# Attention and two feed-forward layers on one core: other PSUM banks, sums spread by TensorE, low halves on VectorE, weights from 16-bit halves

## The chip, the cores and the metric

The kernel runs on 1 core of one Trainium2 chip. The metric is the device time of one execution in microseconds (us); a run gives the median of several executions.

## The reference

```python
scores = scale * np.matmul(q, k.transpose(0, 1, 3, 2))        # 2 x 8 x 768 x 768, D = 64
keep = is_global | is_local                                   # 8 global keys, 96 local ones
scores = np.where(keep, scores - slopes * dist, -1000000000.0)
a = np.exp(scores - np.max(scores, axis=-1, keepdims=True))
a = a / (np.sum(a, axis=-1, keepdims=True) + 1e-09)
x = (a @ v)                                                   # as 1536 tokens x 512
h = x @ w_in                                                  # 512 x 2048
x = (np.maximum(h, 0) + np.log1p(np.exp(-np.abs(h)))) @ w_out # layer 0, 2048 x 512
h = x @ w_in2
out = (h / (1 + np.exp(-1.702 * h))) @ w_out2                 # layer 1
```

The weights of the two layers come as 64-bit doubles. Products are made of fp32 values split in a high and a low part: high by high, high by low and low by high.

## The kernel before

**Attention** goes over 12 blocks of 128 queries (n), each in two halves of 4 heads (g = 0, 1), so 24 halves s. `split_attention` is a loop of ns + 3 = 27 iterations whose order is written out by hand: each engine runs its instructions in the order in which the code issues them. Iteration s works on four halves at once:

- TensorE (PE): the scores of s + 1; in odd iterations `turn_r`, the turned 1/sum of a block; `turn`, the transposes of the weights of s - 1; the turned k or q of block n + 2; `values`, the product with v of s - 2. So an iteration runs from one start of scores to the next.
- VectorE (DVE): `reduce(s + 1)`, which adds the bias to the scores and takes their minimum; the low parts kl (even) and ql (odd); in even iterations `weigh` (1/sum, L503 and L504) of block n - 1 and `normalise` (output by 1/sum, L519) of block n - 2 with the high part of x (L526); steps of the converter.
- ScalarE (ACT): the high parts kh and qh, the exponentials of s (`weights_of`), and the copies out of PSUM: turned weights (`copy_p`, L587) and 1/sum (`copy_r`, L514).
- GpSimd (POOL): 1/sum spread over 64 columns (L506), the low part of x (L527), and moves within kh and kl.

Even iterations are those with g = 0. In this text block n of attention is "a block of queries" and a slice of the weights "a weight block".

**The eight PSUM banks** during attention before: four that rotate (`h_pool`, scores take two at a time and the feed-forward layer one), two for the turned weights, one for the outputs (`ps_o`), one for turned q, k and 1/sum (`ps_q`).

**The converter** puts together the fp32 high and low parts of the weights from the doubles, 32 weight blocks of 128 x 1024, by the steps of `split`: t (L142), its scaling on ScalarE (L144), the remaining bits `rest` (L146, L148), the sign (L152), the high part w (L156 on VectorE for the first six weight blocks, L159 on ScalarE for the others), a mask (L160), and the low part (L162). `pump` issues steps while a budget lasts; during attention, with `later` set, ScalarE's part waits in `hold` until the end of an iteration or the next step that empties it. Weight blocks 0 to 5 of layer 0 are put together during attention, the others in layer 0 and 1.

**The feed-forward layers** are 96 units of 12 matmuls into h (`first`) and 12 into four accumulators (`second`), `bend` between them. The first unit's matmuls stand inside attention's last iterations, in four pieces (chunks).

## Time and profile before

| | |
|---|---|
| median of 3 runs | 653.48 us (653.38 to 653.83) |
| profiled execution | 654.91 us, its span 653.3 us |
| PE busy | 623.5 us of the span |
| DVE busy | 411.0 us |
| ACT busy | 362.4 us |
| POOL busy | 50.7 us |

Busy time is an average over stages with different limits, so the rows below cut the span where the work changes: the attention loop, its end, and the layers. A row of the timeline has the start, the length, the operation with what it writes and reads, and in brackets how long the engine was idle before it and what released it. An operation's length holds some overlap with the next one on its engine, so what one costs in a busy engine is the distance from its start to the next one's start.

### The profile page before, as it was taken

Reading aid. Unit: us, or ns where it says so; the run is one execution under the profiler, and the core shown is the slowest. Engines: PE = TensorE matmul, PEld = TensorE weight load, DVE = VectorE, ACT = ScalarE, POOL = GpSimd, SP = SyncE. Lnnn points to the kernel's source line nnn. Section 1 sums busy time; section 2 is a strip of 40 time slices with the busy share of each in tenths; the row PEclk is TensorE's granted clock in tenths of the full one; section 3 lists DMA queues with packets and bytes.
Section 4 is the critical chain, followed back from the end, with each engine's and each line's share of the span. In section 5 each row is a group of like instructions: output and inputs, shape, how many; then the busy total and the mean of one; then the engine's idle time right before and its main releaser. Section 6 shows DMA issues by size and latency. Waiting matters only on the chain.

```text
span 653.3 us, 8758 instructions
## 1 busy us (share of the span) xinstructions
PE 623.5 (95%) x3290; PEld 508.1 (78%) x3290; DVE 411.0 (63%) x752; ACT 362.4 (55%) x676; POOL 50.7 (8%) x70
## 2 busy tenths in 40 slices
PE   7889788899999999999999999999999999999995
PEld 4677676688788778888888888888888888888884
DVE  5988978989999976899867997674121111211111
ACT  4988997576887666777666763443222222222221
POOL 3224442100000000000000003000000000000000
PEclk9899999999999999999999999999999999999998
DMA  9877657950100001530005671000010000100002
GB/s 227 160 187 172 127 142 230 330 205 0 65 1 2 0 1 64 194 130 0 1 0 194 207 245 65 0 1 0 1 65 0 1 1 1 64 2 0 1 1 70
DMA packets 65715, 51.51 MB, mean 79 GB/s; under 512 B 41920, under 2 KB 58304, under 8 KB 65664
## 3 DMA queue, kind: packets, MB, share of 16 engines
q1 hardware_dynamic: 65376, 50.86, 26.5%
q8 instruction: 28, 0.46, 0.3%
q14 instruction: 23, 0.19, 0.1%
q10 hardware_dynamic: 288, 0.00, 0.0%
HBM read 44.70 MB, written 4.19 MB: 75 GB/s over the span
## 4 chain that ended last, share of the span: by engine, by line
PE 74%; DVE 18%; ACT 4%; issue 3%; DMA 1%; ACTq 0%; DVEq 0%
PE h L238 33%; PE acc L292 20%; PE acc L290 13%; DVE t L152 2%; PE t L580 2%; DVE w L162 2%; PE s L543 2%; PE o L602 2%; PE qps L461 2%; DVE g L252 2%; DVE gl L259 1%; DVE pr L556 1%; DVE rest L146 1%; DVE rest L148 1%; DVE g L246 1%
## 5 line engine op out<-in xcount | busy, mean ns | idle before, releaser
L259 DVE TENSOR_TENSOR gl<-g,gh 128x512 fp32r<-128x512 f32 x96 | 67.1, 699 | 165.7 <-ACT gh L257 165.6
L290 PE MATMUL acc<-gh,w 128*128 128x512 f32 x384 | 126.6, 390 | 0.0
L292 PE MATMUL acc<-w,gh 128*128 128x512 f32 x384 | 125.5, 389 | 0.0
L257 ACT ACTIVATE gh<-g 128x512 fp32r<-128x512 f32 x96 | 60.4, 629 | 93.9 <-PE acc L292 80.0
L290 PEld LDWEIGHTS acc<-gh,w 128*128 128x128 f32 x384 | 72.1, 188 | 15.5 <-ACT e L269 0.3
L292 PEld LDWEIGHTS acc<-w,gh 128*128 128x128 f32 x384 | 72.1, 188 | 14.9
L265 ACT ACTIVATE g<-h 128x512 f32<-128x512 f32 x48 | 28.7, 598 | 93.8 <-PE h L238 76.2
L290 PE MATMUL acc<-gl,w 128*128 128x512 f32 x192 | 74.9, 390 | 0.6 <-DVE gl L259 0.6
L292 PE MATMUL acc<-w,gl 128*128 128x512 f32 x192 | 74.8, 390 | 0.0
L268 ACT ACTIVATE e<-h 128x512 f32<-128x512 f32 x48 | 28.4, 592 | 33.8 <-PE h L238 30.8
L238 PE MATMUL h<-x0h,w 128*128 128x512 f32 x128 | 44.8, 406 | 2.4 <-DVE g L254 2.4
L568 ACT ACTIVATE pr<-pr,mins 128x256 f32<-128x256 f32 (+1 forms) x96 | 45.7, 484 | 1.2 <-DVE mins L556 1.2
L238 PE MATMUL h<-x1h,w 128*128 128x512 f32 x128 | 42.7, 393 | 0.6 <-DVE g L254 0.6
L144 ACT ACTIVATE t<-t,ebias 128x1024 int32<-128x1024 int32 x32 | 36.7, 1146 | 10.9 <-DVE t L142 10.8
L290 PEld LDWEIGHTS acc<-gl,w 128*128 128x128 f32 x192 | 36.0, 188 | 8.6 <-DVE gl L259 1.2
L292 PEld LDWEIGHTS acc<-w,gl 128*128 128x128 f32 x192 | 36.0, 188 | 8.0 <-DVE gl L259 0.5
L238 PE MATMUL h<-x2h,w 128*128 128x512 f32 x128 | 42.0, 389 | 0.0
L238 PE MATMUL h<-y1h,w 128*128 128x512 f32 x128 | 42.0, 389 | 0.0
L238 PE MATMUL h<-y2h,w 128*128 128x512 f32 x128 | 42.0, 389 | 0.0
L238 PE MATMUL h<-y0h,w 128*128 128x512 f32 x128 | 42.0, 389 | 0.0
L148 DVE SCALAR_TENSOR_TENSOR rest<-raw,rest 128x1024 int32<-128x1024 int32 x32 | 39.8, 1245 | 0.2
L246 DVE SCALAR_TENSOR_TENSOR g<-c,g 128x512 f32<-128x512 f32 x48 | 32.8, 684 | 10.7 <-ACT g L272 10.7
(125 smaller groups left out, 1150.6 us busy)
## 6 DMA issues: line engine op xcount, KB each, us to landing
raw<-in_moe_w_in SPq DMA_DIRECT2D x32, 512.0 KB, 4.8
raw<-in_moe_w_out SPq DMA_DIRECT2D x32, 512.0 KB, 5.6
kn<-in_k SPq DMA_DIRECT2D x12, 256.0 KB, 4.3
qn<-in_q SPq DMA_DIRECT2D x12, 256.0 KB, 4.7
vn<-in_v SPq DMA_DIRECT2D x12, 256.0 KB, 3.4
out<-o SPq DMA_DIRECT2D x12, 256.0 KB, 2.1
vp<-vn SPq DMA_DIRECT2D x10, 192.0 KB, 3.8
part<-o SPq DMA_DIRECT2D x2, 512.0 KB, 2.8
```

What stands on the lines that cost most here:

```text
L144: s["hold"].append(lambda: nc.scalar.activation(t, t, AF.Relu, bias=ebias, scale=float(2 ** 12)))
L148: nc.vector.scalar_tensor_tensor(rest, low, 17, rest, op0=ALU.logical_shift_right, op1=ALU.bitwise_or)
L152: nc.vector.scalar_tensor_tensor(t, top, -2 ** 31, t, op0=ALU.bitwise_and, op1=ALU.bitwise_or)
L238: nc.tensor.matmul(h, lhsT=w[:, a, c * P:(c + 1) * P], rhs=b[:, c, :], start=c == 0 and n == 0, stop=c == KD - 1 and n == 2)
L246: nc.vector.scalar_tensor_tensor(st[u - 1]["g"], st[u - 1]["c"], -1.0, st[u - 1]["g"], op0=ALU.add, op1=ALU.subtract)
L257: nc.scalar.activation(gh, g, AF.Copy)
L259: nc.vector.tensor_tensor(gl, g, gh.bitcast(F32), op=ALU.subtract)
L265: nc.scalar.activation(g, s["h"], AF.Gelu_apprx_sigmoid)
L268: nc.scalar.activation(e, s["h"], AF.Abs)
L290: nc.tensor.matmul(o, lhsT=wo[:, a, ms], rhs=g, **kw)
L292: nc.tensor.matmul(o, lhsT=g[:, ms], rhs=wo[:, a, :], **kw)
L568: nc.scalar.activation(pr[:, j, e, :w], pr[:, j, e, :w], AF.Exp, bias=mins[:, H * n + h:H * n + h + 1], scale=-1.0, accum_out=sums[n][:, h ...
```

## The change

- **PSUM.** The four rotating banks become four named ones, h0 to h3, one buffer each. Scores use h0 and h1 every time, before one pair of four in turn. Turned q, k and 1/sum use h2 and h3 in turn. The bank set free goes to `ps_o`, which has two. The layers' h goes through the four in the order of `BANKS`.
- **Sums.** 1/sum is no longer spread by GpSimd and then turned with 4 transposes; 8 matmuls of TensorE do both, with 1/sum broadcast over 64 columns against the identity.
- **Low half of x** on VectorE. `normalise` with both halves of x stands ahead of `weigh`, kl and `reduce`, and behind the converter's first steps.
- **Weights.** `rest` is put together by two operations, each writing one 16-bit half of a word. The high part w is copied by ScalarE for all weight blocks. In attention a step that needs ScalarE's result is issued only after the `flush` at the end of an iteration. The declared costs are 640 for 680.
- `reduce(0)` stands ahead of the loop; the first unit's chunks are issued in three iterations, not four; the last iterations' budget is half.

```diff
+BANKS = (2, 0, 1, 3)
...
     def split(s):
         raw = s.pop("raw")
-        top, low = raw[:, :, 1], raw[:, :, 0]
+        top, half = raw[:, :, 1], raw.bitcast(U16).rearrange("p m (two h) -> p m two h", two=2)
         t = conv.tile([P, NW2], I32, tag="t", name="t")
         nc.vector.tensor_scalar(t, top, 0x7FFFFFFF, 9, op0=ALU.bitwise_and, op1=ALU.logical_shift_right)
-        yield 680
+        yield 640
         s["hold"].append(lambda: nc.scalar.activation(t, t, AF.Relu, bias=ebias, scale=float(2 ** 12)))
         rest = conv.tile([P, NW2], I32, tag="t", name="rest")
-        nc.vector.tensor_scalar(rest, top, 0x1FF, 15, op0=ALU.bitwise_and, op1=ALU.logical_shift_left)
-        yield 680
-        nc.vector.scalar_tensor_tensor(rest, low, 17, rest, op0=ALU.logical_shift_right, op1=ALU.bitwise_or)
-        yield 1210
-        while s["hold"]:
-            s["hold"].pop()()
+        part = rest.bitcast(U16).rearrange("p (m h) -> p m h", h=2)
+        nc.vector.tensor_scalar(part[:, :, 0], half[:, :, 0, 1], 0xFFFF, None, op0=ALU.bitwise_and)
+        yield 640
+        nc.vector.tensor_scalar(part[:, :, 1], half[:, :, 1, 0], 0x1FF, None, op0=ALU.bitwise_and)
+        yield 640
+        yield None
         nc.vector.scalar_tensor_tensor(t, top, -2 ** 31, t, op0=ALU.bitwise_and, op1=ALU.bitwise_or)
         w = s["pool"].tile([P, 2, NW2], F32R, tag=s["tag"], name=s["name"])
+        s["hold"].append(lambda: nc.scalar.activation(w[:, 0, :], t.bitcast(F32), AF.Copy))
         yield 1210
-        if s["early"]:
-            nc.vector.tensor_copy(w[:, 0, :], t.bitcast(F32))
-            yield 640
-        else:
-            nc.scalar.activation(w[:, 0, :], t.bitcast(F32), AF.Copy)
+        yield None
         nc.vector.tensor_scalar(t, t, -2 ** 23, None, op0=ALU.bitwise_and)
-        yield 680
-        nc.vector.scalar_tensor_tensor(w[:, 1, :], rest, 2.0 ** -35, t.bitcast(F32), op0=ALU.mult, op1=ALU.mult)
+        yield 640
+        nc.vector.scalar_tensor_tensor(w[:, 1, :], rest, 2.0 ** -36, t.bitcast(F32), op0=ALU.mult, op1=ALU.mult)
         s["w"] = w
         yield 1210
...
         def run(self):
             while self.queue:
                 yield from split(self.queue.pop(0))
+            yield 0
         def step(self):
-            cost = next(self.ops, None)
+
+            if self.stuck and self.hold:
+                return None
+            self.stuck = False
+            cost = next(self.ops, 0)
+            if cost == 0:
+                self.ops = self.run()
+                cost = next(self.ops)
             if cost is None:
-                self.ops = self.run()
-                cost = next(self.ops, None)
+                self.stuck = True
+                return self.step()
             if not self.later:
                 self.flush()
             return cost
...
             self.credit += budget
             while self.credit > 0:
                 cost = self.step()
+                if cost is None:
+                    break
                 self.credit = self.credit - cost if cost else 0
         def flush(self):
             while self.hold:
-                self.hold.pop()()
+                self.hold.pop(0)()
         def finish(self, s):
             while "w" not in s:
-                self.step()
+                if self.step() is None:
+                    self.flush()
     def ffn_phase(x1, slots, work, h_pool, weights, converter):
...
                 if u not in st:
-                st[u] = {"h": h_pool.tile([P, TB], F32, tag="h", name="h")}
+                st[u] = {"h": h_pool.tile([P, TB], F32, tag=f"h{BANKS[u % 4]}", name="h")}
             h = st[u]["h"]
             for c in chunks:
                 for n, (a, b) in enumerate(((0, xh), (0, xl), (1, xh))):
...
         ps_t = pool("ps_t", 1, space=PSUM)
-        ps_o = pool("ps_o", 1, space=PSUM)
-        ps_q = pool("ps_q", 1, space=PSUM)
+        ps_o = pool("ps_o", 2, space=PSUM)
+        turns = []
...
                 nc.sync.dma_start(t[WIN:P], v[b, :, 0:GLB, :].rearrange("h p d -> p h d"))
                 vs[n].insert(0, t)
-        def turned(src, early=False):
-            t = (ps_o if early else ps_q).tile([P, NP, P], F32, tag="o" if early else "q", name="qps")
+        def bank(last=False):
+
+            turns.append(h_pool.tile([P, TB], F32, tag=f"h{3 if last else 2 + len(turns) % 2}", name="qps"))
+            return turns[-1].rearrange("p (c k) -> p c k", c=NP)
+
+        def turned(src):
+            t = bank()
             src = src.rearrange("p h d -> p (h d)")
             for p in range(NP):
                 nc.tensor.transpose(t[:, p, :], src[:, p * P:(p + 1) * P], ident)
...
             nc.vector.tensor_scalar(sums[n], sums[n], 1e-9, None, op0=ALU.add)
             nc.vector.reciprocal(sums[n], sums[n])
-            r = s_pool.tile([P, H, D], F32, tag="r", name="r", bufs=1)
-            nc.gpsimd.tensor_scalar(r, sums.pop(n).to_broadcast([P, H, D]), 1.0, 1.0, op0=ALU.mult, op1=ALU.mult)
-            rts[n] = r
         def turn_r(n):
-            rts[n] = turned(rts[n])
+
+            r = sums.pop(n)
+            t = rts[n] = bank(n >= nb - 3)
+            for p in range(NP):
+                for e in range(2):
+                    nc.tensor.matmul(t[e * D:(e + 1) * D, p, :], lhsT=r[:, 2 * p + e, :].to_broadcast([P, D]),
+                                     rhs=ident, start=True, stop=True)
         def copy_r(n):
-            rt = s_pool.tile([P, NP, P], F32, tag="rt", name="rt", bufs=1)
-            nc.scalar.activation(rt, rts[n], AF.Copy)
-            rts[n] = rt
+            y = s_pool.tile([P, NP, P], F32, tag="y", name="y")
+            nc.scalar.activation(y, rts[n], AF.Copy)
+            rts[n] = y
         def normalise(n):
-            y = ys[n] = rts.pop(n)
-            nc.vector.tensor_tensor(y, outs.pop(n), y, op=ALU.mult)
-
-        def split_x(n):
             b, i = blocks[n]
             t0 = b * S + i * P
             hi, lo = (x[:, :, t0 % TB:t0 % TB + P] for x in x1[t0 // TB])
-            y = ys.pop(n)
+            y = rts.pop(n)
+            nc.vector.tensor_tensor(y, outs.pop(n), y, op=ALU.mult)
             nc.vector.tensor_copy(hi, y)
-            nc.gpsimd.tensor_tensor(lo, y, hi.bitcast(F32), op=ALU.subtract)
+            nc.vector.tensor_tensor(lo, y, hi.bitcast(F32), op=ALU.subtract)
...
             i = blocks[n][1]
             w, at = (NW, own(i) - WIN - GLB) if i else (P, own(0))
             qh, ql = qts[n]
-            banks = [h_pool.tile([P, TB], F32, tag="h", name=f"s{e}") for e in range(2)]
+            banks = [h_pool.tile([P, TB], F32, tag=f"h{e}", name=f"s{e}") for e in range(2)]
             ps[s] = ([x.rearrange("p (j k) -> p j k", j=2) for x in banks], w)
             for j in range(2):
                 for m, (a, c) in enumerate(((qh, kh), (qh, kl), (ql, kh))):
...
         yield
         scores(0)
         spin(2)
+        reduce(0)
         for s in range(ns + 3):
             n, g = divmod(s, 2)
             live = n < nb
...
                 turn(s - 1)
             if s == 0:
-                reduce(0)
                 bias(bias_0, d0, 4)
                 weights_of(0)
                 run(split_k(1), split_q(1))
...
                     weights_of(s)
                 if s == 1:
                     bias(bias_w, dw, 4)
+                if s > 1:
+                    converter.pump(budget // 2)
+                if g == 0 and 0 <= n - 2 < nb:
+                    normalise(n - 2)
                 if g == 0 and 0 <= n - 1 < nb:
                     weigh(n - 1)
-                if s > 1:
-                    converter.pump(budget // 2)
                 run(kept)
                 if s + 1 < ns:
                     reduce(s + 1)
                 if s == 4:
                     check_counts()
-                if g == 0 and 0 <= n - 2 < nb:
-                    normalise(n - 2)
-                    split_x(n - 2)
+                converter.pump(budget // 2 * g if s + 1 < ns else budget)
                 if g == 1 and 0 <= n - 1 < nb:
                     copy_r(n - 1)
-                converter.pump(budget // 2 * g if s + 1 < ns else 2 * budget)
                 if s >= 1 and s - 1 < ns:
                     copy_p(s - 1)
             converter.flush()
...
             if s >= 2 and s - 2 < ns:
                 values(s - 2)
-            if ns - 5 <= s < ns - 1:
-                first(0, [s - ns + 5])
+            if ns - 4 <= s < ns - 1:
+                first(0, ((0,), (1,), (2, 3))[s - ns + 4])
             if ns - 1 <= s < ns + 2:
                 bend(s - ns + 1)
                 if s < ns + 1:
```

**Place 1: VectorE in the even iteration s = 8.** The rows start at the first step of it that is not a reduction; of the eight rows of `reduce` (L556 before, L570 after) one stands. Before (s_747 are scores, o the output in PSUM, rest, t and raw_1 the converter's tiles, x0h and x0l the halves of x):

```order
L148 SCALAR_TENSOR_TENSOR rest<-raw_1_291,rest 128x1024 [waits DVE_49]
L503 TENSOR_SCALAR sum<-sum 128x8 [waits Activation_49]
L504 RECIPROCAL sum<-sum 128x8 [waits DVE_49]
L490 TENSOR_TENSOR kl<-qps,kh 128x4x128 [waits Activation_49]
L556 ISA pr,mins<-s_747,bias_w 128x256 [waits PE_49]
...
L519 TENSOR_TENSOR rt<-o,rt 128x512 [waits Pool_49]
L526 CAST x0h<-rt 128x4x128 [waits DVE_49]
L152 SCALAR_TENSOR_TENSOR t<-raw_1_291,t 128x1024
```

After:

```order
L158 TENSOR_SCALAR t<-t 128x1024 [waits Activation_49]
L160 SCALAR_TENSOR_TENSOR w_1_723<-rest,t 128x1024 [waits DVE_49]
L539 TENSOR_TENSOR y<-o,y 128x512 [waits PE_49]
L540 CAST x0h<-y 128x4x128 [waits DVE_49]
L541 TENSOR_TENSOR x0l<-y,x0h 128x4x128 [waits DVE_49]
L517 TENSOR_SCALAR sum<-sum 128x8
L518 RECIPROCAL sum<-sum 128x8 [waits DVE_49]
L504 TENSOR_TENSOR kl<-qps,kh 128x4x128 [waits Activation_49]
L570 ISA pr,mins<-s_753,bias_w 128x256 [waits PE_49]
```

`normalise` (L519, now L539) went from behind the reduction to ahead of it, with the low half (L541) behind it, and the converter's mask (L158) and low part (L160) of weight block 1, which the order before reaches later, stand ahead of all; the mask waits for ScalarE.

**Place 2: ScalarE at the end of s = 6 and in s = 7.** Before:

```order
L476 ACTIVATE qh<-qps 128x512 [waits PE_49]
L568 ACTIVATE pr,sum<-pr,mins 128x256 [waits DVE_49] x4
L514 ACTIVATE rt<-qps 128x512 [waits PE_49,Pool_49]
L587 ACTIVATE pt<-t 128x1024 [waits PE_49,Activation_49]
L144 ACTIVATE t<-t,ebias 128x1024
L488 ACTIVATE kh<-qps 128x4x128 [waits PE_49]
L568 ACTIVATE pr,sum<-pr,mins 128x256 [waits DVE_49] x4
```

After (y is 1/sum in SBUF, w_1_723 the high part of weight block 1):

```order
L490 ACTIVATE qh<-qps 128x512 [waits PE_49]
L582 ACTIVATE pr,sum<-pr,mins 128x256 [waits DVE_49] x4
L531 ACTIVATE y<-qps 128x512 [waits PE_49]
L601 ACTIVATE pt<-t 128x1024 [waits PE_49,Activation_49]
L155 ACTIVATE w_1_723<-t 128x1024 [waits DMAHW4_49,DMAHW3_49,DVE_49]
L502 ACTIVATE kh<-qps 128x4x128 [waits PE_49]
L582 ACTIVATE pr,sum<-pr,mins 128x256 [waits DVE_49] x4
```

In s = 7 the scaling of t stood between the copy of the turned weights (pt) and kh; now the copy of w (L155) stands there, and the scaling is earlier.

**Place 3: VectorE at the end of attention**, ahead of the first units' bends (g and e). Before:

```order
L142 TENSOR_SCALAR t<-raw_5_1631 128x1024 [waits DMAHW2_49,DMAHW1_49]
L146 TENSOR_SCALAR rest<-raw_5_1631 128x1024
L148 SCALAR_TENSOR_TENSOR rest<-raw_5_1631,rest 128x1024 [waits DVE_49]
L246 SCALAR_TENSOR_TENSOR g<-c,g 128x512 [waits Activation_49]
L152 SCALAR_TENSOR_TENSOR t<-raw_5_1631,t 128x1024 [waits Activation_49]
L156 CAST w_5_1814<-t 128x1024 [waits DVE_49]
L160 TENSOR_SCALAR t<-t 128x1024 [waits DVE_49]
L162 SCALAR_TENSOR_TENSOR w_5_1814<-rest,t 128x1024 [waits DVE_49]
L246 SCALAR_TENSOR_TENSOR g<-c,g 128x512 [waits Activation_49]
L252 SCALAR_TENSOR_TENSOR g<-g,e 128x512
L252 SCALAR_TENSOR_TENSOR g<-g,e 128x512 [waits DVE_49]
L254 SCALAR_TENSOR_TENSOR g<-h,g 128x512 [waits DVE_49] x2
```

After:

```order
L153 SCALAR_TENSOR_TENSOR t<-raw_5_1406,t 128x1024 [waits Activation_49]
L158 TENSOR_SCALAR t<-t 128x1024 [waits Activation_49]
L160 SCALAR_TENSOR_TENSOR w_5_1748<-rest,t 128x1024 [waits DVE_49]
L539 TENSOR_TENSOR y<-o,y 128x512 [waits PE_49,Activation_49]
L540 CAST x2h<-y 128x4x128 [waits DVE_49]
L541 TENSOR_TENSOR x2l<-y,x2h 128x4x128 [waits DVE_49]
L517 TENSOR_SCALAR sum<-sum 128x8
L518 RECIPROCAL sum<-sum 128x8 [waits DVE_49]
L255 SCALAR_TENSOR_TENSOR g<-c,g 128x512 [waits Activation_49] x2
L261 SCALAR_TENSOR_TENSOR g<-g,e 128x512 [waits DVE_49] x2
L263 SCALAR_TENSOR_TENSOR g<-h,g 128x512 [waits DVE_49] x2
```

Before, the whole of weight block 5 (raw_5) stands here; after, its last three steps, and three operations on x.

## Rows read from the trace of the kernel before

**Rows 1.** Stages: from:to, length, busy us (instructions) per engine, granted PE clock, DMA.

```profile
27.85:106.24 78.39, 66.90 (x735) 55.26 (x733) 67.61 (x227) 68.81 (x194) 30.17 (x35) 1.00 0.66 159
106.24:128.98 22.74, 18.62 (x148) 14.88 (x147) 21.60 (x40) 14.09 (x30) 4.88 (x4) 1.00 0.92 310
128.98:133.09 4.11, 4.11 (x12) 3.02 (x12) 2.81 (x6) 4.11 (x8) 1.16 (x1) 0.58 0.55 208
133.09:235.00 101.91, 100.69 (x439) 81.52 (x438) 99.63 (x139) 74.04 (x111) 0.12 (x1) 1.00 0.12 42
235.00:645.50 410.50, 410.45 (x1810) 339.23 (x1808) 199.72 (x271) 183.79 (x283) 5.94 (x4) 1.00 0.15 50
```

**Rows 2.** TensorE in time, one odd and one even half: start, us, operation, idle before.

```profile
32.75 0.39 PE L543 MATMUL s<-kh,qh 64*128 64x256 f32 x2
...
33.67 0.66 PE L461 MATMUL qps<-ident,r 128*128 128x128 f32 x4
34.16 1.04 PE L580 MATMUL t<-ident,pr 128*128 128x128 f32 x8
...
36.68 0.39 PE L543 MATMUL s<-kh,qh 64*128 64x256 f32 x2
...
37.59 1.09 PE L580 MATMUL t<-ident,pr 128*128 128x128 f32 x8
...
39.94 0.44 PE L602 MATMUL o<-pt,vp 128*64 128x128 f32 x4 [0.81 <-PE qps L461]
...
40.96 0.39 PE L543 MATMUL s<-kh,qh 64*128 64x256 f32 x2
```

**Rows 3.** VectorE in time, in the even half.

```profile
36.29 0.16 DVE L503 TENSOR_SCALAR sum<-sum 128x8 f32<-128x8 f32 x1
...
36.61 0.65 DVE L142 TENSOR_SCALAR t<-raw 128x1024 int32<-128x1024 int32 x1
37.18 0.68 DVE L490 TENSOR_TENSOR kl<-qps,kh 128x512 fp32r<-128x512 f32 x1
37.78 0.41 DVE L556 CUSTOM_DVE_ANT_0 pr<-s,bias_w 128x256 f32<-128x256 f32 x1
...
39.15 0.68 DVE L519 TENSOR_TENSOR rt<-o,rt 128x512 f32<-128x512 f32 x1
39.87 0.43 DVE L526 CAST x0h<-rt 128x512 fp32r<-128x512 f32 x1
40.21 0.68 DVE L146 TENSOR_SCALAR rest<-raw 128x1024 int32<-128x1024 int32 x1
```

**Rows 4.** GpSimd in time, in the same even half.

```profile
40.38 1.66 POOL L527 TENSOR_TENSOR x0l<-rt,x0h 128x512 fp32r<-128x512 f32 x1 [2.12 <-DVE x0h L526]
```

**Rows 5.** VectorE by line while layer 0 runs: count, busy, mean ns, idle.

```profile
L148 DVE SCALAR_TENSOR_TENSOR rest<-raw,rest 128x1024 int32<-128x1024 int32 x10 | 12.2, 1217 | 0.0
...
L142 DVE TENSOR_SCALAR t<-raw 128x1024 int32<-128x1024 int32 x10 | 6.8, 682 | 0.0
```

**Rows 6.** ScalarE by line: the later weight blocks' copy.

```profile
L159 ACT ACTIVATE w<-t 128x1024 fp32r<-128x1024 f32 x10 | 10.6, 1056 | 2.2 <-DVE t L152 1.8 <-DVE rest L148 0.4
```

**Rows 7.** ScalarE in time, in the odd half.

```profile
34.42 0.60 ACT L514 ACTIVATE rt<-qps 128x512 f32<-128x512 f32 x1 [0.96 <-PE qps L461]
35.30 1.03 ACT L587 ACTIVATE pt<-t 128x1024 f32<-128x1024 f32 x1 [0.28 <-PE t L580]
36.22 0.59 ACT L488 ACTIVATE kh<-qps 128x512 fp32r<-128x512 f32 x1
```

**Rows 8.** TensorE in time, in the first halves.

```profile
15.12 0.63 PE L461 MATMUL qps<-ident,qn 128*128 128x128 f32 x4 [1.70 <-DVE mins L556]
```

**Rows 9.** TensorE in time: the first product after attention.

```profile
128.98 0.50 PE L238 MATMUL h<-x0h,w 128*128 128x512 f32 x1 [2.42 <-DVE g L254]
```

**Rows 10.** TensorE in time: a wait in layer 0.

```profile
229.37 0.50 PE L290 MATMUL acc<-gl,w 128*128 128x512 f32 x1 [0.58 <-DVE gl L259]
```

**Rows 11.** Granted clock in short stretches, columns as in the first group.

```profile
16.00:18.00 2.00, 1.94 (x16) 0.75 (x12) 1.52 (x6) 1.98 (x9) 0.00 (x0) 0.69 1.15 333
18.00:20.00 2.00, 2.00 (x10) 1.67 (x10) 1.97 (x9) 0.87 (x2) 0.00 (x0) 0.50 1.40 226
```

**Rows 12.** TensorE in time: one wait in the loop.

```profile
31.73 0.44 PE L602 MATMUL o<-pt,vp 128*64 128x128 f32 x4 [1.45 <-issue]
```

More of the change, by code (lines that the diff above doesn't have):

```diff
@@ L12 @@
 I32 = mybir.dt.int32
-U32 = mybir.dt.uint32
+U16 = mybir.dt.uint16
 AF = mybir.ActivationFunctionType
@@ L128, in load_words, with load_weights @@
                           sources[l][1].bitcast(I32)[f * P:(f + 1) * P, :])
-    def load_weights(pool, l, f, early=False):
+    def load_weights(pool, l, f):
         raw = pool.tile([P, NW2, 2], I32, tag=f"w{f}", name=f"raw{l}_{f}")
         load_words(raw, l, f)
-        return {"raw": raw, "pool": pool, "tag": f"w{f}", "name": f"w{l}_{f}", "early": early}
+        return {"raw": raw, "pool": pool, "tag": f"w{f}", "name": f"w{l}_{f}"}
     def split(s):
         raw = s.pop("raw")
-        top, low = raw[:, :, 1], raw[:, :, 0]
+        top, half = raw[:, :, 1], raw.bitcast(U16).rearrange("p m (two h) -> p m two h", two=2)
@@ L171, in __init__ @@
             self.queue, self.ops, self.credit, self.blocks, self.hold = [], iter(()), 0, [], []
-            self.later = later
+            self.later, self.stuck = later, False
         def add(self, s):
@@ L436, in split_attention @@
         raw, qts, vs = {}, {}, {}
-        ps, prs, pts, outs, sums, rts, ys = {}, {}, {}, {}, {}, {}, {}
+        ps, prs, pts, outs, sums, rts = {}, {}, {}, {}, {}, {}
         def load(n):
@@ L469, in turn_q @@
         def turn_q(n):
-            qts[n] = turned(raw[n]["qn"], n < 2)
+            qts[n] = turned(raw[n]["qn"])
         def split_q(n):
@@ L485, in split_k @@
             i = blocks[n][1]
-            t = raw[n]["kn"]
+            t = raw.pop(n)["kn"]
             at = slice(own(i), own(i) + P)
@@ L814, in hidden_pool @@
     def hidden_pool(hctx):
-        return hctx.enter_context(tc.tile_pool(name="h", bufs=4, space=PSUM, reuse_waits="tile"))
+        return hctx.enter_context(tc.tile_pool(name="h", bufs=1, space=PSUM, reuse_waits="tile"))
     with ExitStack() as wctx:
@@ L831, in attention_two_ffns @@
                     f = len(weights)
-                    weights[0, f] = load_weights(wa_pool, 0, f, early=True)
+                    weights[0, f] = load_weights(wa_pool, 0, f)
                     converter.add(weights[0, f])
```

## Prediction

> **What bounds the kernel now.** I read the stages first [rows 1], cut at starts of scores. From 235 to 645.5 TensorE is busy 410.45 of 410.50 us: nothing here shortens its matmuls, so that stage stays. From 133.09 to 235 VectorE is busy 99.63 of 101.91 us beside TensorE's 100.69: nearly a tie, in which VectorE makes TensorE wait now and then. From 106.24 to 128.98 TensorE is busy 18.62 of 22.74 and VectorE 21.60: VectorE bounds, with weight blocks left over. The short stage behind it runs at a granted clock of 0.58 of full speed. The loop, 78.39 us, has no full engine (PE 66.90, DVE 67.61, ACT 68.81), so there the chain of waits counts. It holds iterations 4 to 21, nine even and nine odd: 4.36 us each on average.
>
> Then the timeline of TensorE [rows 2]. The odd iteration from 32.75 has no wait and takes 3.93 us. The even one from 36.68 takes 4.28, of which 0.81 is a wait ahead of `values`. The row names the turned q as releaser, but `normalise` on VectorE (L519) runs from 39.15 to 39.83 [rows 3], 0.11 before `values` start: the single output bank is the cause. TensorE's own even work is 4.28 - 0.81 = 3.47.
>
> **The change part by part.** *Two output banks* take away the 0.81, if nothing else ends last. *One pair of banks for scores* puts another wait there: scores of s + 2 need `reduce(s + 1)` finished, where before VectorE could be an iteration late. In even iterations `reduce` now has `normalise`, both halves of x, `weigh` and kl ahead of it, and `normalise` can't start before the last `values`, which end as the iteration starts. By distances of starts [rows 3]: `normalise` 0.72, high half 0.34, `weigh` 0.32, kl 0.60, reduction 1.37. The low half leaves GpSimd, where it takes 1.66 [rows 4]; on VectorE I take kl's 0.60, the same kind of subtraction (bounds 0.60 and the 0.72 of `normalise`). The sum is 3.95, and with two hand-overs between engines of 0.11 to 0.2 some 4.3: as long as now. TensorE's 3.47 lies beside it, so the gain of the second bank is used up. Nine pairs of 3.93 + 4.3 are 74.1 us; what 78.39 holds above that is converter work.
>
> *The sums* take 8 matmuls of 64 columns for 4 transposes (33.67 to 34.16, 0.49) [rows 2]. Sixteen of the same width in `values` take 40.96 - 39.94 = 1.02, so 8 take 0.51: nothing (bounds 0 and 0.5 in each odd iteration, 4.5 in all, if each costs as much as a transpose). The spread on GpSimd that is removed lay beside other work. Turned q, k and sums in two banks, and the layers' order of four banks: nothing, since each bank is read by ScalarE and VectorE within an iteration and comes back two turns later; without that cover a turn would wait, at most by the 0.6 of a copy.
>
> *The weights.* `rest` was L146, of L142's form, and L148: 0.68 + 1.22 [rows 5]. Now it is two operations of one source on 16-bit halves with a step. No row shows such a one: between 0.68 (like L142, one source from SBUF) and 1.22 (like L148, one element per cycle), a little of either end thinkable. I take 0.68, as they are L142's kind with the same count of elements: 0.54 saved per weight block. The copy of w leaves VectorE in attention (about L142's 0.65) for ScalarE, 1.06 [rows 6]. A page on this: the Trainium skill, VectorE: DVE Perf Modes, "What auto-detection actually checks", has values packed only at a step of one, but two ports for a single source in SBUF; by that the operation costs what L142 costs, and the sum would be the same.
>
> *The new wait in the loop.* ScalarE's copy of w comes behind the copy of the turned weights at an odd iteration's end, ahead of kh (place 2 of the change), and the mask (L158) heads VectorE's next even iteration (place 1). In the odd iteration of [rows 7] the turned weights wait for TensorE (0.28) and kh starts at 36.22: the copy would end at 36.22 + 1.06 = 37.28, 0.60 after the even iteration starts at 36.68; where ScalarE is later, up to 0.9. I take 0.75 (bounds 0 and 0.9). Behind the mask stand `normalise`, `weigh`, kl and `reduce`, and TensorE's scores wait for all of these. With the mask's 0.57 (as L142, 36.61 to 37.18) `normalise` starts at 1.32 in place of some 0.15: 1.2 late, in iterations 12, 16 and 20. In 4 and 8 the low part of w (1.22) stands ahead too: 2.4 late. Together 3 x 1.2 + 2 x 2.4 = 8.4 (bounds 0 and 10). One of two chunks of the first unit in the loop stands in an odd iteration, against which nothing waits: three matmuls, 0.7. The loop is then 74.1 + 8.4 + 0.7 = 83.2, **+4.8**.
>
> *Ahead of the loop* TensorE waits 1.70 for the first reductions [rows 8]; `reduce(0)` now stands earlier: **-1.0** (0 to -1.7).
>
> *The end of attention.* Since the loop has taken in more weight steps, place 3 shows 3 steps of weight block 5 (1.22 + 0.68 + 1.22 = 3.1) where 7 stood (6.4 by these durations, the copy at 0.65); weight block 4 is wholly ahead. Low halves add 0.6 each. So VectorE no longer bounds, and the 22.74 - 18.62 = 4.1 of TensorE's idle time goes, of which 2.42 stands ahead of the second unit [rows 9]: **-4.1** (bounds -2 and -4.1). The 4.11 us at 0.58 follow that wait: 4.11 x 0.42 = 1.7 of full clock are lost, **-1.7** (0 to -1.7).
>
> *Layer 0.* TensorE's idle time is 101.91 - 100.69 = 1.22, or, at the next stage's 410.5 / 1810 us per record, 101.91 - 439 x 0.2268 = 2.35; one wait on VectorE is 0.58 [rows 10]. Ten weight blocks at 0.54 free 5.4 us of VectorE: **-1.5** (0 to -2.4). Layer 1: nothing, VectorE is half idle.
>
> *The clock.* The five lengthened even iterations leave TensorE idle for 4.3 + 1.2 - 3.47 = 2.0, or 3.2. After 1.70 at the start it ran at 0.69 and 0.50 [rows 11], after 2.42 at 0.58, after 1.45 in the loop [rows 12] at 1.00 [rows 1]. I take it that the two of 3.2 lower the clock and the three of 2.0 don't, for the work around them is dense. One costs 1.7 at most; the next even iteration has 0.8 of slack, which covers half a microsecond of it: 1.25 each, **+2.5** (bounds 0 and 5 x 1.7 = 8.5). The Trainium skill, TensorE: Matmul & The Clock Gate, "HAM oscillation — how this bites in real kernels", says that a wait which comes back in every round puts the array to half clock each time, and so speaks against this change; the row of 1.45 at 1.00 shows that a shorter one in this loop does not, and no row here has one of 2.0 in it.
>
> **Sum.** 4.8 - 1.0 - 4.1 - 1.7 - 1.5 + 2.5 = -1.0. The profiled execution, 654.91, would become 653.9. It lies 1.43 above the median of the runs, 653.48; by the same difference these come to **652.5 us**. A measurement of this kernel can tell about 0.2%, 1.3 us, from no change: the forecast is no change that can be told.
>
> **Rivals.**
>
> *The copy is hidden* (mask and low part of w fall into time that VectorE has spare). The floor is then VectorE's own time: 67.6, plus 9 low halves 5.4, less four weight blocks at 0.54 + 0.65 (4.8), plus one and a half weight blocks more in the loop at 5.2 (7.8): 76.0, with waits about 77. 77 - 78.4 = -1.4, and -1.0 - 4.1 - 1.7 - 1.5: -9.7, **644**. For it: ScalarE waits 0.96 and 0.28 in the odd iteration, so work fits in. Against it: the copy can't start before the turned weights are copied, and these come from TensorE.
>
> *Every lengthened iteration drops the clock* (slower). All five waits, 2.0 and 3.2, are above the 1.70 after which the first iterations ran at half clock, and each costs the whole 1.7: 8.5 for 2.5, **658.5**; with the slack taken off 656. It decides from waits of 2.0 on. Against it: those at the start had matmuls for the start-up ahead of them, not a loop.
>
> *No drop at all*: 2.5 less, **650.0**.
>
> *The 16-bit halves cost 1.22 each*: 0.54 more per weight block, not less. VectorE's 99.6 in layer 0 becomes 105.0, TensorE follows at +3 to +5 for -1.5, and the loop's mask comes later by some 1 to 2: **659.5**. For it: a step of two words in the source, as in L148; against: L142 reads with the same step of 64 bits and takes 0.68. No row has a 16-bit destination.
>
> **How the numbers follow.** Forecast 0.40 (649.5 to 655 by its own bounds); copy hidden 0.22; five drops 0.18; no drop 0.10; slow halves 0.10. Faster: 0.12 of the forecast (short waits, whole gain in layer 0), 0.22, 0.09 of no drop, 0.01: 0.44. Same: 0.17 + 0.03 + 0.01 + 0.01 = 0.22. Slower: 0.11 of the forecast, 0.15, 0.08: 0.34. The range of 643.5 to 658.5 leaves out the slow halves and the outer ends of copy hidden and five drops, 0.2 in all.
>
> **What would show it.** The start of the scores of s = 23 at 110.0 (106.24 now); even iterations of 4.3 us, of 5.5 with the mask ahead and 6.7 with the low part too, with TensorE's idle time ahead of scores and released by the last minima; the mask's wait put down to ScalarE's copy; the 16-bit operations at 0.68; no wait ahead of the second unit; a granted clock under 1.00 behind iterations 4 and 8 and at no other place from 27.85 on. I am wrong low if the clock falls at 2.0 us of waiting, and wrong high if the mask never waits.

## The result and the profile after

The changed kernel takes 661.93 us (median of 4 runs, 660.95 to 664.62) against 653.6: a ratio of 1.0134, with a 95% interval of 1.0104 to 1.0164. It is slower, and outside the predicted range of 643.5 to 658.5. Its profiled execution takes 662.22 us with a span of 660.2, against 654.91 and 653.3: 6.9 us of span to find.

The stages of the kernel after, cut at the same places of the program as [rows 1] as far as they go (loop, end of attention, layers; same columns):

```profile
27.54:120.88 93.34, 78.06 (x840) 65.38 (x838) 76.15 (x240) 74.81 (x201) 5.52 (x14) 0.93 0.56 134
120.88:140.00 19.12, 19.12 (x171) 15.43 (x171) 13.77 (x35) 15.49 (x32) 0.00 (x0) 1.00 0.91 307
140.00:237.00 97.00, 96.96 (x425) 78.85 (x424) 95.03 (x139) 75.30 (x114) 0.00 (x0) 1.00 0.18 65
237.00:652.50 415.50, 415.50 (x1835) 344.17 (x1834) 194.74 (x273) 185.67 (x285) 7.07 (x4) 1.00 0.14 49
```

The loop went from 78.39 to 93.34, at a mean granted clock of 0.93. From its end on TensorE waits for nothing: that part of the span is 660.2 - 120.88 = 539.3, against 653.3 - 106.24 = 547.1. So the change lost 14.6 us up to the scores of s = 23 and won 7.7 behind them.

What TensorE waited for from 8 to 140 us, first before, then after (who waits, for whom, us in total, times, longest):

```profile
PE o L602 <- issue: 8.6, 7, 1.4
...
PE o L602 <- PE qps L461: 1.8, 3, 0.8
...
PE o L602 <- DVE rt L519: 0.5, 1, 0.5
```

```profile
PE s L557 <- DVE mins L570: 12.2, 9, 3.6
PE s L557 <- POOL kh L512: 1.6, 1, 1.6
PE s L557 <- ACT pr L582: 1.5, 1, 1.5
PE h L247 <- DVE kl L504: 1.2, 1, 1.2
...
```

The single output bank had cost 10.9 us in eleven waits, under three names: "issue" and the turned q stand where the true releaser, `normalise`, was not the last by the profile; it ended 0.1 us before each of the eight between 31 and 91 us. After, these are gone, and 12.2 us in nine waits of the scores for the minima stand in their place, 10.9 of it in the loop. The next three rows are one wait each, in iterations 14, 12 and 20; in 12 it is the reduction again that ends just ahead of the scores (75.75 for 75.90). The longest wait for the minima, 3.6 us, ends iteration 4 (stretches of iterations 4 to 7; columns as above):

```profile
27.54:34.59 7.05, 3.46 (x43) 2.95 (x41) 5.76 (x15) 5.75 (x16) 0.99 (x2) 1.00 0.79 228
34.59:40.87 6.28, 6.28 (x56) 5.38 (x56) 4.67 (x19) 3.18 (x9) 0.00 (x0) 0.73 0.43 82
40.87:44.99 4.12, 3.46 (x42) 2.94 (x41) 3.83 (x13) 4.12 (x12) 0.00 (x0) 1.00 0.69 161
44.99:49.65 4.66, 4.66 (x56) 3.92 (x56) 3.31 (x12) 4.25 (x13) 0.00 (x0) 1.00 0.50 87
```

Iteration 4 lasts 7.05 for 3.46 of TensorE's work, and iteration 5 behind it runs at a clock of 0.73. The next two, without converter steps at their head, are 4.12 and 4.66. ScalarE and VectorE in iteration 4:

```profile
27.61 1.05 ACT L155 ACTIVATE w<-t 128x1024 fp32r<-128x1024 f32 x1
```

```profile
28.69 0.79 DVE L158 TENSOR_SCALAR t<-t 128x1024 int32<-128x1024 int32 x1 [2.07 <-ACT w L155]
29.51 1.22 DVE L160 SCALAR_TENSOR_TENSOR w<-rest,t 128x1024 fp32r<-128x1024 int32 x1
30.65 0.68 DVE L539 TENSOR_TENSOR y<-o,y 128x512 f32<-128x512 f32 x1
```

VectorE waits 2.07 for the copy of w, does the mask and the low part, and comes to the normalisation 3.1 us into the iteration; the reduction follows from 33.33 on and the scores at 34.59. TensorE in the odd iteration 7 after, beside [rows 2]:

```profile
44.99 0.64 PE L557 MATMUL s<-kh,qh 64*128 64x256 f32 x2 [0.66 <-DVE mins L570]
...
46.14 1.09 PE L526 MATMUL qps<-ident,sum 128*64 128x128 f32 x16
47.17 1.09 PE L594 MATMUL t<-ident,pr 128*128 128x128 f32 x8
```

The sums take 47.17 - 46.14 = 1.03, where the four transposes took 0.49: the profile counts 16 matmuls for the 8 of the code. The scores in front of them, which stand behind a wait, take 1.15 for 0.92. Last, the operations on 16-bit halves in layer 0, beside [rows 5]:

```profile
L148 DVE TENSOR_SCALAR rest<-raw 128x1024 uint16<-128x1024 uint16 x10 | 7.7, 771 | 0.0
L150 DVE TENSOR_SCALAR rest<-raw 128x1024 uint16<-128x1024 uint16 x10 | 7.7, 768 | 0.0
```

At 0.77 they are near the lower bound of 0.68, not 1.22. The Trainium skill, VectorE: DVE Perf Modes, "What auto-detection actually checks", has a step on 16-bit values forbid the packing but not the use of two ports by a single source in SBUF; by that rule the rate is L142's, and these rows agree but for 0.09.

### The profile page after: what moved, and what is told of

Its sections match the earlier page's. It is cut to its first block, busy times and chain, and to the rows that moved or that the text cites. A ratio compares the mean times of both kernels' runs of the same rounds, so it can differ in the third digit from the quotient of the medians.

```text
span 660.2 us, 8983 instructions
## 1 busy us (share of the span) xinstructions
PE 634.2 (96%) x3434; PEld 519.4 (79%) x3434; DVE 399.3 (60%) x758; ACT 369.3 (56%) x682; POOL 20.2 (3%) x46
## 4 chain that ended last, share of the span: by engine, by line
PE 88%; DVE 6%; ACT 2%; issue 2%; DMA 1%; POOL 0%; ACTq 0%; DVEq 0%; POOLq 0%
PE h L247 40%; PE acc L299 20%; PE acc L301 20%; PE s L557 3%; PE qps L526 2%; PE t L594 2%; DVE pr L570 1%; PE o L616 1%; ACT w L155 1%; DVE y L539 1%; DVE kl L504 1%; DMA ints<-in_n_local 1%; DVE t L158 1%; PE qps L475 1%; DVE x0l L541 0%
## 5 line engine op out<-in xcount | busy, mean ns | idle before, releaser
L247 PE MATMUL h<-x0h,w 128*128 128x512 f32 x128 | 43.1, 395 | 1.2 <-DVE kl L504 1.2
L155 ACT ACTIVATE w<-t 128x1024 fp32r<-128x1024 f32 x32 | 33.9, 1058 | 18.2 <-DVE t L153 15.2
L299 PEld LDWEIGHTS acc<-gl,w 128*128 128x128 f32 x192 | 36.1, 188 | 8.8 <-DVE gl L268 1.4
L301 PEld LDWEIGHTS acc<-w,gl 128*128 128x128 f32 x192 | 36.1, 188 | 7.4
L153 DVE SCALAR_TENSOR_TENSOR t<-raw,t 128x1024 int32<-128x1024 int32 x32 | 40.2, 1256 | 2.2 <-ACT t L145 2.2
```

The lines of the kernel that those rows point to most:

```text
L153: nc.vector.scalar_tensor_tensor(t, top, -2 ** 31, t, op0=ALU.bitwise_and, op1=ALU.bitwise_or)
L155: s["hold"].append(lambda: nc.scalar.activation(w[:, 0, :], t.bitcast(F32), AF.Copy))
L247: nc.tensor.matmul(h, lhsT=w[:, a, c * P:(c + 1) * P], rhs=b[:, c, :], start=c == 0 and n == 0, stop=c == KD - 1 and n == 2)
L299: nc.tensor.matmul(o, lhsT=wo[:, a, ms], rhs=g, **kw)
L301: nc.tensor.matmul(o, lhsT=g[:, ms], rhs=wo[:, a, :], **kw)
```

## The experiments

Twelve kernels; all ratios are to the kernel before, timed on the same chip in the same session. "Scores 23" is the start of the scores of s = 23 in the profiled run, "behind" what is left of the span.

| kernel | median us | ratio (interval) | scores 23 | behind |
|---|---|---|---|---|
| before | 653.6 | 1 | 106.24 | 547.1 |
| changed | 661.93 | 1.0134 (1.0104 to 1.0164) | 120.88 | 539.3 |
| e1 sums on GpSimd | 656.68 | 1.0060 (1.0037 to 1.0083) | 114.78 | 537.9 |
| e2 copy on VectorE | 651.33 | 0.9977 (0.9964 to 0.9989) | 109.02 | 539.3 |
| e3 steps behind | 653.65 | 1.0004 (0.9991 to 1.0017) | 112.54 | 539.2 |
| e4 wait filled | 657.58 | 1.0067 (1.0044 to 1.0089) | 116.06 | 539.4 |
| e5 before + halves | 650.17 | 0.9958 (0.9944 to 0.9972) | 107.15 | 540.3 |
| e6 = e1 and e2 | 647.03 | 0.9905 (0.9885 to 0.9926) | 107.01 | 538.6 |
| e7 = e6, normalise behind | 642.95 | 0.9851 (0.9832 to 0.9870) | 101.53 | 538.8 |
| e8 before + banks | 642.51 | 0.9839 (0.9820 to 0.9859) | 98.39 | 544.4 |
| e9 changed, normalise behind | 650.73 | 0.9958 (0.9942 to 0.9973) | 110.88 | 539.4 |
| e10 before + banks + halves | 640.25 | 0.9800 (0.9777 to 0.9823) | 97.74 | 540.5 |
| e11 = e7, low half on GpSimd | 641.20 | 0.9822 (0.9796 to 0.9848) | 100.36 | 538.9 |
| e12 = e10, low q first | 644.24 | 0.9861 (0.9842 to 0.9879) | 101.85 | 540.5 |

**e1: the sums undone.**

```diff
+            nc.gpsimd.tensor_scalar(r, sums.pop(n).to_broadcast([P, H, D]), 1.0, 1.0, op0=ALU.mult, op1=ALU.mult)
...
-                    nc.tensor.matmul(t[e * D:(e + 1) * D, p, :], lhsT=r[:, 2 * p + e, :].to_broadcast([P, D]),
+            rts[n] = turned(rts[n], n >= nb - 3)
```

> The changed kernel with one part undone: 1/sum is again spread over 64 columns by GpSimd and turned with four transposes. Theory (the eight matmuls of the sums cost 1.02 us in each odd iteration, where TensorE is what everything waits for, against 0.49 for four transposes): each of the 12 blocks saves 0.5 us, odd iterations go from 4.66 to about 4.1, the scores of s = 23 start 5 to 6 us earlier, and the time is 656 us (changed kernel: 661.9). Rival (TensorE's matmuls are hidden behind VectorE's chain): no change, 661 to 662. The waits of 3.6, 2.8 and 2.3 us in iterations 4, 8 and 16 and the half clock behind them stay by both.

Medians fall by 5.3, scores 23 by 6.1, and the odd iteration 7 from 4.66 to 4.08. As the theory has it, but for the clock: in e1's profiled run it falls to 0.54 and 0.70 behind iterations 4 and 8 and stays at 1.00 behind 16, so that the 5.3 is not the sums alone. The clean reading is the odd iterations at full clock in both: 7, 13, 15, 19 and 21 are 0.58 shorter each.

**e2: the copy of w undone**, for the first six weight blocks.

```diff
-        s["hold"].append(lambda: nc.scalar.activation(w[:, 0, :], t.bitcast(F32), AF.Copy))
+            nc.vector.tensor_copy(w[:, 0, :], t.bitcast(F32))
```

> The changed kernel with one part undone: the high part of the first six weight blocks is copied by VectorE, so that the mask waits for no ScalarE. Theory (the mask's wait for ScalarE heads VectorE's even iterations and holds up everything behind it): even iterations 4, 8 and 16 go from 7.05, 6.51 and 5.78 to 4.2 to 5, TensorE never waits over 1.5 us there, so the half clock in iterations 5, 9 and 17 (6.28, 6.21, 7.58) goes too (4.7 each); 9 to 13 us in all, of which 2 are given back at the end of attention where VectorE has the copies to do: 650 to 655 us. Rival (VectorE is full, and the copy costs there what the wait cost): 659 to 663.

Iterations 4, 8 and 16 take 4.37, 4.12 and 4.23, and 5, 9 and 17 run at 1.00 (4.67, 4.67, 4.65); 10.6 us less. VectorE had room for the copies: the theory holds. Iteration 12 stays long (5.47): there the sign step heads VectorE's list, and it waits for ScalarE too.

```profile
63.31 1.23 DVE L153 SCALAR_TENSOR_TENSOR t<-raw,t 128x1024 int32<-128x1024 int32 x1 [1.84 <-ACT t L145]
```

Iteration 15 falls to a clock of 0.71.

**e3: the steps moved behind the reduction** in even iterations, the copy still on ScalarE.

```diff
-                if s > 1:
+                if s > 1 and (g or s + 1 >= ns):
                     converter.pump(budget // 2)
...
-                converter.pump(budget // 2 * g if s + 1 < ns else budget)
+                converter.pump(budget // 2 * (s > 1) if s + 1 < ns else budget)
```

> The changed kernel with one move: in even iterations the converter's steps are issued behind the reduction and not ahead of the normalisation; the copy of w stays on ScalarE. Theory (it is the place of the mask at the head of the even iteration that costs): all even iterations of the loop take 4.1 to 4.3, no wait of TensorE over 1 us, no half clock; 10 to 14 us faster than the changed kernel, 648 to 652 us. Rival (ScalarE's load with the copies is what lengthens the loop, wherever the mask stands): iterations of 5 to 7 us remain, now the odd ones, and the time stays above 658.

8.3 less than the changed kernel, short of the theory. The even iterations 8, 12 and 16 are 4.12, 3.71 and 4.23, but the odd ones 9, 13 and 17 now 6.68, 5.28 and 5.41: the mask and its wait head those. The clock still falls once, to 0.71 in iteration 15. Both were half right: the wait costs less where TensorE has more work beside it, but it does not vanish.

**e4: the long wait filled with matmuls.**

```diff
+            if s in (4, 8, 16):
+                spin(8)
```

> The changed kernel with eight matmuls of zeros added on TensorE behind the products with v in iterations 4, 8 and 16 (they work on nothing that is used), so that TensorE is not idle through the long wait. Nothing else moves. Theory (the long idle time is what lowers the clock in iterations 5, 9 and 17): these iterations run at a granted clock of 1.00 and take 4.7 us instead of 6.28, 6.21 and 7.58, and the time falls by 5 to 6 us to 656. Rival (the clock falls for another reason, such as the matmuls of the sums): no change in iterations 5, 9 and 17, 661 to 663 us.

```profile
26.95:33.99 7.04, 5.34 (x50) 3.71 (x49) 5.76 (x15) 5.74 (x16) 0.99 (x2) 1.00 0.84 236
33.99:38.65 4.66, 4.66 (x56) 3.92 (x57) 4.56 (x19) 3.17 (x9) 0.00 (x0) 1.00 0.53 99
...
80.41:86.18 5.77, 5.77 (x48) 4.78 (x49) 4.04 (x13) 3.01 (x9) 0.21 (x1) 0.70 0.40 64
```

Iteration 4 is as long as in the changed kernel (7.04), only 1.9 us of its 3.6 us of idle time are filled, and iteration 5 runs at 1.00 in 4.66, as do 9 (4.66) and 17 (4.42). So in these three places the idle time is what lowered the clock. A new stretch at 0.70 in iteration 15 gives 1.5 back; 4.4 us less in all.

**e5: the halves alone**, in the kernel before.

```diff
-        nc.vector.tensor_scalar(rest, top, 0x1FF, 15, op0=ALU.bitwise_and, op1=ALU.logical_shift_left)
-        nc.vector.scalar_tensor_tensor(rest, low, 17, rest, op0=ALU.logical_shift_right, op1=ALU.bitwise_or)
+        nc.vector.tensor_scalar(part[:, :, 0], half[:, :, 0, 1], 0xFFFF, None, op0=ALU.bitwise_and)
+        nc.vector.tensor_scalar(part[:, :, 1], half[:, :, 1, 0], 0x1FF, None, op0=ALU.bitwise_and)
```

> The kernel before with one part of the change alone: the remaining bits of the weights come from two operations on 16-bit halves (0.63 us each from start to start in the changed kernel) in place of L146 and L148 (0.6 and 1.13). Theory (this part is a gain on VectorE, felt only where VectorE bounds: the end of attention and layer 0): half a microsecond per weight block, the loop as before, some 1 us at the end of attention and up to 1.5 in layer 0: 1 to 2.5 us faster than before. Rival (VectorE's saving is hidden everywhere): no difference.

2.9 less, a little over the theory's range, all of it behind scores 23 (the profiled run, 649.33, is the second fastest of seven, and that of before is slower than all its other runs, so that their profiles lie further apart). The end of attention and the start of layer 0 there, to set beside [rows 1]:

```profile
107.00:130.00 23.00, 21.36 (x159) 16.70 (x159) 20.89 (x41) 16.79 (x37) 4.86 (x4) 1.00 0.93 312
130.00:134.00 4.00, 4.00 (x19) 3.29 (x18) 2.92 (x7) 2.99 (x6) 1.30 (x1) 1.00 0.72 231
134.00:235.00 101.00, 100.03 (x441) 82.49 (x440) 95.22 (x138) 77.47 (x117) 0.00 (x0) 1.00 0.11 40
```

TensorE is idle for 1.6 us of the 23.00, for 4.1 of 22.74 before, and the stage behind it runs at 1.00 for 0.58.

**e6: e1 and e2 together.**

> The changed kernel with both costly parts undone: sums spread by GpSimd with four transposes, and the first six weight blocks' high part copied by VectorE. Theory (the two costs lie on different iterations and add up): odd iterations 4.1, even ones 4.1 to 5, the scores of s = 23 start near 104 (120.9 in the changed kernel, 106.2 before), and the stages behind that are those of the changed kernel: 644 to 647 us. Rival (once the sums are cheaper, VectorE, busy 74.7 of 82.0 us in the loop with its own copies, bounds it): 649 to 651, as with the copy alone.

647.03: e1's gain still comes on top of e2's (4.3), the theory's sum. Scores 23 stand at 107.0 for 104, with one stretch at 0.67 in iteration 13 and one at 0.52 ahead of the loop.

**e7: e6 with the normalisation behind the reduction.**

```diff
-                if g == 0 and 0 <= n - 2 < nb:
-                    normalise(n - 2)
                 if g == 0 and 0 <= n - 1 < nb:
                     weigh(n - 1)
                 run(kept)
                 if s + 1 < ns:
                     reduce(s + 1)
+                if g == 0 and 0 <= n - 2 < nb:
+                    normalise(n - 2)
```

> The kernel of the run with both costly parts undone, and the normalisation with both halves of x behind the reduction again. Theory (in the even iterations the chain of normalisation, halves, sums, kl and reduction ends last, since there is one pair of banks for scores, and holds TensorE for 0.65 us): even iterations without converter steps go from 4.1 to 3.5, and the time falls by 2 to 4 us against that kernel, unless VectorE's sum of work (about 75 us for the loop) is what bounds it: then no difference, and the waits move to other iterations.

4.1 less: even iterations without steps are 3.4. Part of the 4.1 is the clock: the profiles lie 5.2 us apart, of which e6 loses 1.5 ahead of the loop, at 0.52, and 1.1 in iteration 13, at 0.67, where e7 ran at 1.00; that leaves between 2 and 3 for the move.

**e8: the banks alone**, in the kernel before (with the chunks in three iterations).

```diff
-        ps_o = pool("ps_o", 1, space=PSUM)
-        ps_q = pool("ps_q", 1, space=PSUM)
+        ps_o = pool("ps_o", 2, space=PSUM)
...
-            banks = [h_pool.tile([P, TB], F32, tag="h", name=f"s{e}") for e in range(2)]
+            banks = [h_pool.tile([P, TB], F32, tag=f"h{e}", name=f"s{e}") for e in range(2)]
```

> The kernel before with the PSUM banks of the change alone (one pair for scores, two for turned blocks, two for outputs), with the first unit's chunks in three iterations as those banks need; the normalisation stays behind the reduction, the low half of x on GpSimd. Theory (the banks themselves cost nothing; what costs is the order on VectorE that the change puts with them): the 0.8 us wait of the products with v goes, even iterations take 3.5 to 4.3, and the time is 0 to 4 us less than before. Rival (a single pair for scores makes TensorE wait for each reduction, converter steps ahead of it included): even iterations of 4.3 to 5, 2 to 6 us slower than before.

10.5 less, far over the theory's 0 to 4. TensorE's waits from 8 to 140 us there:

```profile
PE h L239 <- ACT rt L520: 2.1, 1, 2.1
PE s L549 <- DVE mins L562: 2.0, 5, 0.6
PE qps L467 <- DVE ql L484: 1.6, 5, 0.5
```

No wait for the output bank is left of 10.9 us, and one pair for scores costs 2.0, half of it ahead of the loop. With `reduce` ahead of `normalise`, the single pair is hardly a price.

**e9: the changed kernel with only the normalisation moved** (the diff of e7).

> The changed kernel with one move: the normalisation with both halves of x stands behind the reduction, as before; sums on TensorE and the copy of w on ScalarE stay, the mask still heads the even iterations. Theory (the place ahead of the reduction costs 1.7 us of the chain in each even iteration, of which TensorE feels what exceeds its own work): even iterations without steps 3.5 for 4.1, iterations 4, 8 and 16 at 5.4, 4.9 and 4.1 for 7.05, 6.51 and 5.78, and with waits under 2 us no half clock in the loop: 12 to 14 us less than the changed kernel, 648 to 650. Rival (the mask's wait for ScalarE carries the cost by itself): the long iterations and the half clock stay, 657 to 660.

11.2 less than the changed kernel, 0.8 short of the theory's least: even iterations without steps are 3.4, and 4, 8 and 16 are 5.26, 5.17 and 5.16, but the clock still falls to 0.72 and 0.73 in 5 and 9, behind waits of 1.8 and 1.7. On the clock the rival was right.

**e10: banks and halves alone.**

> The kernel before with two parts of the change, the PSUM banks and the weights from 16-bit halves, and nothing else. Theory (the two gains, 10.5 and 2.9 us when each stands alone, lie in different places, the loop's TensorE waits and VectorE's share at the end of attention and in layer 0): they add up for the most part, 639 to 641 us. Rival (both take away the same VectorE waits): 642, as with the banks alone.

640.25, 2.0% faster than the kernel before and the lowest median of all: 0.9839 x 0.9958 = 0.980, so within the intervals the two gains add up in full.

**e11: e7 with the low half of x on GpSimd.**

> The kernel of the run with both costly parts undone and the normalisation behind, and the low half of x on GpSimd again. Theory (in that kernel the turned k waited up to 1.8 us for the low part of q on VectorE, which stands behind the low half of x): 0.6 us off VectorE in each block, up to 4 us less than the 642.95 of that kernel: 639 to 641. Rival (GpSimd's 1.66 us subtraction slows VectorE beside it or is waited for at the end): no difference.

641.20, 1.75 less, and TensorE's waits for the low part of q fall from 5.7 to 3.5, as the theory has it. But the intervals of e7 and e11 overlap, so that a gain is not shown.

**e12: e10 with the low part of q first.**

```diff
+                if g == 1:
+                    run(kept)
                 if s > 1:
                     converter.pump(budget // 2)
                 run(kept)
```

> The kernel before with the banks and the 16-bit halves, and one move: in odd iterations the low part of q stands ahead of the converter's steps on VectorE. In the run with banks and halves the turned k waited for it (1.07, 1.25, 0.58 and 0.36 us), because the bank that the turned k takes is the one that the low part of q still reads. Theory (that wait is what the two banks for turned blocks cost): the four waits go, 1 to 3 us less than the 640.25 of that kernel, 637.5 to 639.5. Rival (a step that is put behind the low part of q makes the reduction late by the same time, and TensorE waits there): no difference.

The theory fell. TensorE's waits in e10, then in e12:

```profile
PE qps L468 <- DVE ql L485: 3.6, 5, 1.3
...
PE s L550 <- DVE mins L563: 1.1, 3, 0.5
```

```profile
PE s L550 <- DVE mins L563: 5.8, 11, 1.2
```

The waits for the low part of q (3.6) went, and waits for the minima rose from 1.1 to 5.8; the median is 4.0 us longer. The order alone does not do that, since ql and the first share of the steps stand ahead of the reduction in both kernels. What differs is how long the steps take: behind ql they start while GpSimd works on the low half of x. One step in e12 beside it, and the same step with GpSimd idle:

```profile
33.51 1.27 POOL L534 TENSOR_TENSOR x0l<-rt,x0h 128x512 fp32r<-128x512 f32 x1 [3.40 <-DVE x0h L533]
```

```profile
33.94 1.92 DVE L164 SCALAR_TENSOR_TENSOR w<-rest,t 128x1024 fp32r<-128x1024 int32 x1
...
53.52 1.23 DVE L164 SCALAR_TENSOR_TENSOR w<-rest,t 128x1024 fp32r<-128x1024 int32 x1
```

The loop's converter steps, 27 in either kernel, take 24.1 us in e10 and 28.0 in e12. Eight of e12's and one of e10's start 0.4 to 0.9 us after GpSimd's low half of x and are 0.3 to 1.1 us longer than the same step elsewhere; ql beside the same work keeps its 0.68. That GpSimd is what holds the steps is read from these rows; no run takes its work away from them.

## Why the prediction was wrong

Its sum in us of span, by its own terms, and what the profiles show:

| term | forecast | measured |
|---|---|---|
| even iterations of the loop | 47.1 (4.3, 5.5, 6.7) | 45.9 |
| odd iterations at full clock (with the chunk) | 36.1 | 41.3 |
| half clock in the loop | +2.5 | +6.1 |
| ahead of the loop | -1.0 | -0.3 |
| end of attention, its clock, layer 0 | -7.3 | -7.7 |
| all against before | -1.0 | +6.9 |

**Right, to about a microsecond: the lengthened even iterations.** Normal ones 4.12 for 4.3; 4, 8, 12, 16 and 20 at 7.05, 6.51, 4.84, 5.78 and 5.24 for 6.7, 6.7, 5.5, 5.5 and 5.5, by the mechanism named: the mask waits for ScalarE's copy at the head of VectorE's list (e2 takes it away in 4, 8, 16 and 20), and the normalisation stands in the chain ahead of the scores (e9). The copy ended 1.12 us into iterations 4 and 16 and 0.68 into 8, 12 and 20, for 0.75 with a bound of 0.9. In 20 TensorE waits for kl in that chain, ahead of the first unit's chunk. That the second output bank's gain is used up in the changed kernel is right too: 10.9 us of waits went, 12.2 came. Right also, in sum, the end of attention and layer 0, though the measured -7.7 contains two blocks' sums. The start of scores 23 named as a sign, 110.0, leaves out the sum's own +2.5 for the clock; with it the forecast was 112.5, against 120.88.

**The step that failed first: the price of the sums.** The prediction gave eight matmuls 0.51 us, because it read 16 rows of `values` in 1.02 as sixteen matmuls. The code of `values` issues eight; the profile counts two for each. By the right reading the same 1.02 was the price of eight. At +0.5 in each odd iteration, where TensorE bounds, it is 4.8 us in the loop and 1.1 behind it; e1 gives 0.58 back in each of five odd iterations at full clock, and 5.3 in the median. (The bound written down, 0.5 each, 4.5 in all, was the truth.) The other 0.4 of the odd iterations' growth is the slower scores behind a wait, 0.2 each, less what 13 and 15, where the batch changes, lack to the 3.93 that was taken for all.

**The second: the clock.** Two drops at 1.25 were taken, three came, at 6.28 - 4.66 = 1.6, 6.21 - 4.66 = 1.6 and 7.58 - 4.66 = 2.9. The one behind iteration 16 (2.3 us of idle time) was one of the three taken to leave the clock up, and the bound of 1.7 for a drop was too low: it came from a stretch of 4.11 us, while a whole iteration at 0.56 loses 2.9. e4 shows that the idle time is the cause there. The rule cited in the prediction, from the Trainium skill, TensorE: Matmul & The Clock Gate, "HAM oscillation — how this bites in real kernels", agrees with the three long waits here, and not with the short ones, such as the 0.66 ahead of 44.99, behind which it ran at 1.00.

With the odd iterations (4.8 + 0.4), the two sums behind the loop (1.1) and the clock (3.6) as measured, the sum is -1.0 + 4.8 + 0.4 + 1.1 + 3.6 = 8.9, within 2 of the 6.9. What is left: the even iterations were 1.2 shorter than forecast, the end without its sums won 1.5 more, and the place of `reduce(0)` won 0.7 less.

**A step that was right for the wrong scope: the banks.** "The gain of the second bank is used up" held for the change as made, but not of the banks: alone they are the largest gain of all, 10.5 us (e8). What uses it up is the order on VectorE and ScalarE's copy that came along with them. The parts, taken singly from either side: banks -10.5 and halves -2.9 on the kernel before; in the changed kernel, sums 5.3, copy of w 10.6, normalisation ahead 11.2, half clock behind the three long waits 4.4. The last four overlap (the copy and the place of the normalisation make the same long waits, and these the clock), so they don't add up to one figure.

Left open: how much of the 3.6 us that TensorE waits for the low part of q in e10 another place for the steps would win. Its longest wait, 1.25 us, follows a step that took 1.81 us beside GpSimd's low half, for 0.76 elsewhere. The low half of x alone on VectorE, in the kernel before or in e10, was not tried.

## What to carry to other kernels

Price a second buffer by the whole list of waits it removes, under every name they have, and then ask what stands ahead of the next thing that TensorE waits for: here the banks alone won 10.5 us, and the moves on other engines that came along turned that into a loss of 8.3. On an engine that works in order, an instruction that waits for another engine should not stand at the head of the list on which the bounding engine waits: the mask's wait for the copy of w cost 10.6 us here with the clock that it lowered (e2). Before a duration of a group of matmuls is divided by its count, compare the count with the loop in the code.

## What was not expected of the hardware

- The profile shows two matmuls for each fp32 product with v and for each spread of a sum, and one for each fp32 transpose: eight of the first kind take 1.03 us, four of the second 0.49.
- VectorE's converter steps that start while GpSimd works on the low half of x take longer (1.92 for 1.23 us in e12, 1.81 for 0.76 in e10); its subtraction for ql does not.
- Idle time alone does not say whether the granted clock falls. Iteration 14 has 1.60 us of it in the changed kernel and in e4, and 15 behind it ran at 1.00 in the one and at 0.70 in the other. Behind an iteration with 2.5 us idle (5.99 long, 3.46 busy) in e1 it stayed at 1.00, behind one with 1.7 (4.26 long, 2.59 busy) in e2 it fell to 0.71:

```profile
86.24:92.23 5.99, 3.46 (x42) 2.94 (x41) 4.76 (x15) 5.80 (x16) 1.14 (x3) 1.00 0.90 185
92.23:96.30 4.07, 4.07 (x45) 3.50 (x45) 4.07 (x14) 3.17 (x9) 0.00 (x0) 1.00 0.72 249
```

```profile
72.07:76.33 4.26, 2.59 (x31) 2.07 (x29) 4.16 (x14) 3.54 (x13) 2.14 (x6) 1.00 0.64 148
76.33:82.12 5.79, 5.79 (x48) 4.88 (x49) 4.17 (x14) 2.72 (x8) 0.20 (x1) 0.71 0.96 258
```
